# Transposing two streams side by side on half-height TensorE tiles, with loads in 4 KB runs: a scan followed by a mixture of adapters

## The chip, the cores and the metric

The kernel runs on one core of one Trainium2 chip. The metric is device time in microseconds, as a median of several executions; every execution that is compared here was in the fast state (one execution of e7 fell in a second, slower state, at 236.28 us against 232.51 to 234.76 of the other three, and is left out). The "span" that the profile shows is about 2 us shorter than the time. In the tables of the profile PE is TensorE (matmuls), PEld its weight loads, DVE is VectorE, ACT is ScalarE, POOL is GpSimd, SP is SyncE.

## The reference, cut to what matters

```python
# a, b: (8, 6400, 128) float32
for t in range(6400):
    h = a[:, t] * h + b[:, t]          # a recurrence along t, per batch and channel
    x[:, t] = h
x = x.reshape(51200, 128)
logits = x @ w_gate                    # 8 experts
# the two best experts; w = softmax of their two logits
delta = sum over the two of  w * ((x @ A[e]) @ B[e])     # A: 128 x 16, B: 16 x 128
out = x + delta
```

The kernel cuts the 51200 rows into 100 units of 512 rows. For each unit it loads a and b, transposes both on TensorE (channels to partitions, time along the free axis), runs the recurrence as one scan on VectorE, and then works through the adapters: logits, x @ A for all eight experts at once (Z), a multiply by the gates ("mul"), a transpose of the product (T), x itself and the product times B added up in PSUM (R and D), a copy out, a store.

## The kernel before

A small planner in Python gets all operations with estimated durations and dependencies. It decides the order of every engine's queue before the kernel is built, by simulating the engines with a priority for each operation. That matters later, because an operation that waits holds up what stands behind it in the same queue: in the changed kernel the transposes of unit 3, whose data had landed by 11.29 us, started at 20.51 us, behind logits that waited until 18.85 us.

The parts that the change and the argument touch:

```python
# loads: two units in one DMA, 2 KB runs (4 rows of 512 B) in each of 128 partitions; all on SyncE's queue
def load(k):
    u0, n = loads[k]
    s0 = u0 % RING
    for t, rows, ring, last in (("a", a_rows, a_in, "A"), ("b", b_rows, b_in, "B")):
        add_dma(f"ld{t}{k}", "sp", u0 - RING + 2,
            lambda h, rows=rows, ring=ring: h.dma_start(
                ring[:, s0 : s0 + n, :],
                rows[u0 * UT : (u0 + n) * UT, :].rearrange("(n p i) d -> p n (i d)", p=128, i=Q)),
            ...)

# transposes: four of 128 x 128 for a, four for b
def transposes(kind, w):
    ...
        for i in range(Q):
            last = h.transpose(view[:, i, :], ring[:, w % RING, i * 128 : (i + 1) * 128], ident_f[:, :])

# constants: three loads on ScalarE's queue; moe_A comes in 1024 pieces of 64 B
def cst_load(h):
    h.dma_start(cst_f[:, 0:E], moe_w_gate[:, :]).then_inc(s_cst, 16)
    h.dma_start(cst_f[:, E : E + 128].rearrange("p (e r) -> p e r", e=E),
                moe_A.rearrange("e d r -> d e r")).then_inc(s_cst, 16)
    return h.dma_start(cst_f[:, E + 128 : E + 256], moe_B.rearrange("e r d -> (e r) d"))
...
add("cst_in", "act", -109, 1800.0, lambda h: cst_load(h).then_inc(s_cst, 16), ...)
add("cst", "pool", -108, 600.0, lambda h: h.tensor_copy(cst_h[:, :], cst_f[:, :]), ["cst_in"])

# a multiply may run on GpSimd, fed by a copy of z on ScalarE; with PM = 1000 none does
def on_pool(w):
    return w % PM == 3 and 8 < w < NU - 16
...
plan.schedule(390.0)
```

## Time and profile before

The median is 210.99 us (three runs, 210.92 to 211.61).

| read from the profile of before | value |
|---|---|
| span | 209.4 us |
| TensorE busy | 202.2 us (97%), 2842 matmuls |
| VectorE busy | 193.6 us (92%) |
| ScalarE busy | 170.2 us |
| DMA | 393 to 400 GB/s from 40 to 190 us |
| scans start every | 1.94 us (units 20 to 90) |
| last scan starts | 195.0 us, 14.4 us before the end |

The page of the kernel before. The first line is the busy time of each engine with its share of the span and its instructions. The lines with q are DMA queues: packets, MB, share of the 16 DMA engines' time (q1 carries SyncE's loads and stores, q10 ScalarE's queue, q8 the fetches of instructions). The line of shares is the chain of work that ended last. Then come groups of instructions (line, engine, operation, tiles, count, busy us, mean ns, idle time before them), and at the end the DMA issues with the median time from issue to landing.

```profile
PE 202.2 (97%) x2842; PEld 194.9 (93%) x2842; DVE 193.6 (92%) x279; ACT 170.2 (81%) x356; POOL 87.1 (42%) x190
...
q1 hardware_dynamic: 40848, 78.65, 99.8%
q8 instruction: 22, 0.36, 0.7%
...
PE 87%; DVE 6%; ACT 2%; issue 2%; POOL 0%; DVEq 0%; POOLq 0%
...
L555 DVE TENSOR_TENSOR zw<-pZ,g 128x512 f16<-128x512 f32 x100 | 66.9, 674 | 0.8 <-ACT a_st L364 0.2
...
L350 PE MATMUL pA<-ident_f,a_in 128*128 128x128 f32 x400 | 62.2, 279 | 0.8 <-ACT a_st L364 0.6
L350 PE MATMUL pB<-ident_f,b_in 128*128 128x128 f32 x400 | 61.7, 277 | 0.2
...
L406 PE MATMUL pTL<-cst_h,xT 128*128 128x8 f16 x400 | 22.0, 174 | 0.3 <-DVE xT L381 0.3
...
cst_f<-in_moe_A_dram ACTq DMA_DIRECT2D x1, 64.0 KB, 3.9
```

TensorE is busy nearly all the time and 87% of the chain is TensorE. The mean of 279 ns is the time of one transpose from its start to its modelled end; matmuls overlap, so the distance of their starts counts. The timeline of TensorE around 100 us (start, duration, operation) shows it: four transposes of a take 0.44 us of the queue, an f16 block of four takes 0.22 us.

```profile
100.05 0.60 PE L350 MATMUL pA<-ident_f,a_in 128*128 128x128 f32 x4
100.49 0.39 PE L610 MATMUL pO<-cst_h,zwT 128*128 128x128 f16 x4
100.71 0.39 PE L571 MATMUL pTL<-ident_h,zw 128*128 128x128 f16 x4
```

### The profile page before, as it was taken

Reading aid. Unit: us, or ns where it says so; the run is one execution under the profiler, and the core shown is the slowest. Engines: PE = TensorE matmul, PEld = TensorE weight load, DVE = VectorE, ACT = ScalarE, POOL = GpSimd, SP = SyncE. Lnnn points to the kernel's source line nnn. Section 1 sums busy time; section 2 is a strip of 40 time slices with the busy share of each in tenths; the row PEclk is TensorE's granted clock in tenths of the full one; section 3 lists DMA queues with packets and bytes.
Section 4 is the critical chain, followed back from the end, with each engine's and each line's share of the span. In section 5 each row is a group of like instructions: output and inputs, shape, how many; then the busy total and the mean of one; then the engine's idle time right before and its main releaser. Section 6 shows DMA issues by size and latency. Waiting matters only on the chain.

```text
span 209.4 us, 7147 instructions
## 1 busy us (share of the span) xinstructions
PE 202.2 (97%) x2842; PEld 194.9 (93%) x2842; DVE 193.6 (92%) x279; ACT 170.2 (81%) x356; POOL 87.1 (42%) x190
## 2 busy tenths in 40 slices
PE   6989999999999999999999999999999999999992
PEld 4779899999999999999999999999999999999991
DVE  1599999999999999999999999999999999999980
ACT  2437587779888889978979789988998899899993
POOL 1032715063335443563362545435453654354310
PEclk9999999999999999999999999999999999999999
DMA  7999999999999999999999999999999999999677
GB/s 172 388 387 385 389 383 386 385 391 392 398 391 394 399 396 398 401 396 403 391 403 397 399 403 397 398 404 391 398 405 397 405 395 397 402 400 344 237 269 269
DMA packets 42208, 79.23 MB, mean 378 GB/s; under 512 B 3648, under 2 KB 3776, under 8 KB 42176
## 3 DMA queue, kind: packets, MB, share of 16 engines
q1 hardware_dynamic: 40848, 78.65, 99.8%
q8 instruction: 22, 0.36, 0.7%
q10 hardware_dynamic: 1328, 0.14, 0.5%
q14 instruction: 10, 0.08, 0.1%
HBM read 52.56 MB, written 26.21 MB: 376 GB/s over the span
## 4 chain that ended last, share of the span: by engine, by line
PE 87%; DVE 6%; ACT 2%; issue 2%; POOL 0%; DVEq 0%; POOLq 0%
PE pA L350 20%; PE pB L350 19%; PE pO L610 11%; PE pZ L521 10%; PE pO L598 10%; PE pTL L571 10%; DVE xT L381 6%; PE pTL L406 5%; ACT a_st L364 1%; ACT outt L626 1%; PE pB L300 0%; PE pB L303 0%; ACT zwT L590 0%; PE pA L571 0%; PE pB L312 0%
## 5 line engine op out<-in xcount | busy, mean ns | idle before, releaser
L381 DVE TENSOR_TENSOR_SCAN xT<-a_st,xT,pB 128x512 f16<-128x512 f32 x96 | 120.2, 1252 | 2.7 <-PE pB L350 1.1
L364 ACT COPY a_st<-pA 128x512 f32<-128x512 f32 x100 | 59.7, 597 | 18.0 <-PE pA L350 10.7
L555 DVE TENSOR_TENSOR zw<-pZ,g 128x512 f16<-128x512 f32 x100 | 66.9, 674 | 0.8 <-ACT a_st L364 0.2
L626 ACT COPY outt<-pO 128x512 f32<-128x512 f32 x98 | 57.8, 594 | 10.5 <-PE pO L610 9.1
L350 PE MATMUL pA<-ident_f,a_in 128*128 128x128 f32 x400 | 62.2, 279 | 0.8 <-ACT a_st L364 0.6
L350 PE MATMUL pB<-ident_f,b_in 128*128 128x128 f32 x400 | 61.7, 277 | 0.2
L590 ACT COPY zwT<-pTL 128x512 f16<-128x512 f16 x95 | 56.5, 595 | 3.5 <-PE pTL L571 1.9
L350 PEld LDWEIGHTS pB<-ident_f,b_in 128*128 128x128 f32 x400 | 44.1, 142 | 1.8 <-issue 1.1
L350 PEld LDWEIGHTS pA<-ident_f,a_in 128*128 128x128 f32 x400 | 43.3, 143 | 1.8 <-issue 1.3
L610 PE MATMUL pO<-cst_h,zwT 128*128 128x128 f16 x400 | 38.8, 219 | 0.4
L598 PE MATMUL pO<-ident_h,xT 128*128 128x128 f16 x400 | 38.7, 219 | 0.1
L521 PE MATMUL pZ<-cst_h,xT 128*128 128x128 f16 x400 | 38.6, 219 | 0.0
L571 PE MATMUL pTL<-ident_h,zw 128*128 128x128 f16 x380 | 36.7, 219 | 0.0
L598 PEld LDWEIGHTS pO<-ident_h,xT 128*128 128x128 f16 x400 | 30.1, 114 | 0.6 <-ACT outt L626 0.3
L610 PEld LDWEIGHTS pO<-cst_h,zwT 128*128 128x128 f16 x400 | 27.3, 98 | 2.3 <-PE pO L598 0.9
L521 PEld LDWEIGHTS pZ<-cst_h,xT 128*128 128x128 f16 x400 | 28.7, 114 | 0.2
L571 PEld LDWEIGHTS pTL<-ident_h,zw 128*128 128x128 f16 x380 | 25.7, 98 | 0.3
L406 PE MATMUL pTL<-cst_h,xT 128*128 128x8 f16 x400 | 22.0, 174 | 0.3 <-DVE xT L381 0.3
L406 PEld LDWEIGHTS pTL<-cst_h,xT 128*128 128x128 f16 x400 | 20.5, 117 | 0.8 <-DVE xT L381 0.8
L449 POOL TENSOR_TENSOR d_1<-Lg,m_1 128x128 f32<-128x128 f32 (+2 forms) x13 | 5.1, 390 | 32.6 <-DVE m_1 L441 32.6
L449 POOL TENSOR_TENSOR d_0<-Lg,m_0 128x128 f32<-128x128 f32 (+1 forms) x12 | 4.8, 398 | 29.4 <-DVE m_0 L441 29.4
L381 DVE TENSOR_TENSOR_SCAN xT<-a_st,pB 128x512 f16<-128x512 f32 (+1 forms) x8 | 7.5, 942 | 5.7 <-PE pB L350 5.4
(58 smaller groups left out, 129.9 us busy)
## 6 DMA issues: line engine op xcount, KB each, us to landing
a_in<-in_a_dram SPq DMA_DIRECT2D x49, 512.0 KB, 11.4
b_in<-in_b_dram SPq DMA_DIRECT2D x49, 512.0 KB, 11.4
out_dram<-outt SPq DMA_DIRECT2D x49, 512.0 KB, 11.4
a_in<-in_a_dram SPq DMA_DIRECT2D x2, 256.0 KB, 3.6
b_in<-in_b_dram SPq DMA_DIRECT2D x2, 256.0 KB, 4.0
out_dram<-outt SPq DMA_DIRECT2D x2, 256.0 KB, 2.6
cst_f<-in_moe_A_dram ACTq DMA_DIRECT2D x1, 64.0 KB, 3.9
cst_f<-in_moe_B_dram ACTq DMA_DIRECT2D x1, 64.0 KB, 4.5
```

The lines of the kernel that those rows point to most:

```text
L350: last = h.transpose(view[:, i, :], ring[:, w % RING, i * 128 : (i + 1) * 128], ident_f[:, :])
L364: lambda h: h.copy(a_st[w % 2][:, :], pA[:, :]),
L381: last = h.tensor_tensor_scan(out=xT[:, x0 + lo : x0 + hi], data0=a_st[w % 2][:, lo:hi], data1=pB[w % 2][:, lo:hi], initial=init, op0=ALU. ...
L406: last = h.matmul(pL[:, c : c + E], x_block(w, i), wg_h)
L449: lambda h: h.tensor_tensor(out=v(d1[s]), in0=v(Lg[s]), in1=bc(m1[s]), op=ALU.subtract),
L521: last = h.matmul(pZ[w % NZ][:, i * 128 : (i + 1) * 128], x_block(w, i), Acat_h)
L555: lambda h: h.tensor_tensor(out=oview, in0=zview, in1=gview, op=ALU.mult),
L571: last = h.transpose(t_dst(w)[:, i * 128 : (i + 1) * 128], zw[w % 2][:, i, :], ident_h[:, :])
L590: lambda h: h.copy(zwT[w % 2][:, :], t_dst(w)),
L598: last = h.matmul(pO[w % NO][:, i * 128 : (i + 1) * 128], x_block(w, i), ident_h[:, :], start=i == 0, stop=False, skip_group_check=True,)
L610: last = h.matmul(pO[w % NO][:, i * 128 : (i + 1) * 128], zwT[w % 2][:, i * 128 : (i + 1) * 128], Bcat_h, start=False, stop=True, skip_gro ...
L626: return copy(outt[:, w % NOUT, :], pO[w % NO][:, :])
```

## The change

Its intent: a transpose of a 64-row block on the upper half of TensorE and one on the lower half run at the same time. So the unit is laid out as 64 partitions of 8 rows. Unit w of a sits in one half, and unit w of b, shifted by one unit, in the other half, so that the eight pairs of a unit's transposes run side by side. A load of two units fills 128 partitions, in runs of 4 KB instead of 2 KB. Besides, 26 of the 100 multiplies go to GpSimd (with a copy of z on ScalarE for each), the warm-up of TensorE is cut to five matmuls, the planner counts 100 ns for a change between half-height and full-height work, all priorities are new, and the first load of b is issued from ScalarE's queue, so that it is issued sooner.

The diff, cut to its core:

```diff
-    PM = 1000
+    ON_POOL = lambda v: 8 < v < NU - 12 and v % 3 == 1
     ...
-            for i in range(8):
-                for p, dst in ((0, pB[1]), (64, pO[0])):
-                    h.transpose( ... )          # and the rest of the old warm-up
+            for _ in range(5):
+                last = h.matmul(pB[1][:, :], warm_t[:, 0:128], warm_t[:, :])
     ...
+        def place(t, w):
+            shift = 0 if t == "a" else 1
+            half = 64 * ((w + shift) % 2)
+            return (w + shift) // 2, slice(half, half + 64)
+
+        def load(t, n, units, eng="sp"):
+            ring, rows = (a_in, a_rows) if t == "a" else (b_in, b_rows)
+            first, last = place(t, units[0])[1], place(t, units[-1])[1]
+            src = rows[units[0] * UT : (units[-1] + 1) * UT, :]
+            dst = ring[first.start : last.stop, n % RING, :]
+            ...
+                [(dst, src.rearrange("(p i) d -> p (i d)", i=QI))],
     ...
-                for i in range(Q):
-                    last = h.transpose(
-                        view[:, i, :], ring[:, w % RING, i * 128 : (i + 1) * 128], ident_f[:, :]
-                    )
+                for i in range(QI):             # QI = 8
+                    for dst, src, rows in srcs: # a on one half, b on the other
+                        last = h.transpose(dst[:, i, :], src[:, i * D : (i + 1) * D], ident_f[rows, rows])
     ...
-        for k in range(len(loads)):
-            load(k)
+        load("a", 0, [0])
+        load("b", 0, [0], "act")
+        load("a", 0, [1])
+        for n in range(1, NS):
+            load("b", n, [2 * n - 1, 2 * n])
+            load("a", n, [2 * n, 2 * n + 1])
+        load("b", NS, [NU - 1])
     ...
-        plan.schedule(390.0)
+        plan.schedule(410.0)
```

## The prediction

> **What bounds the kernel now.** Three resources are almost equally full, at about 1.9 us per unit of 512 rows (100 units).
> - TensorE: the page has PE 97% busy, and the chain of waits is 87% PE. In the chain between 100 and 125 us the transposes of a and of b take 0.44 us each per unit (4 at 110 ns), the four f16 blocks 0.22 to 0.25 each, the logits 0.11: about 1.88 us.
> - VectorE (timeline): scans 1.19 us and gate multiplies 0.59 us start to start, plus two reductions of 0.19 us per four units: about 1.87 us, with almost no idle time from 14 to 195 us.
> - DMA: 78.65 MB, queue share 99.8%; the table by stretches has 393 to 400 GB/s from 40 to 190 us, so 1.97 us per unit. SyncE's load issues take 1.2 us (median)[...].
>
> Loads run ahead; all have landed by about 185 us, while TensorE still has some ten units to go. From 190 us DMA falls to 270 GB/s. The last scan starts at 195.0 us, the span ends at 209.4.
>
> **What changes.**
> 1. TensorE: 16 half-height transposes in 8 pairs. The warm-up of the old kernel already runs such pairs: both members start together and pairs follow each other every 106 ns, while its 128-column f16 matmuls there take about 102 ns, twice their later 55, so at half clock. At full clock I estimate 53 ns a pair, 0.43 us per unit for both, instead of 0.88. [...] TensorE comes to about 1.6 us per unit.
> 2. VectorE: 26 of the 100 multiplies move to GpSimd: 26 x 0.59 = 15 us less; 1.72 us per unit on average. ScalarE gains 26 copies at 0.48 us (12 us)[...]. Neither becomes a limit.
> 3. DMA: loads in 4 KB packets. In the packet records 64 B take 11 ns, 512 B 27, 2 KB 84, 8 KB 308: about 9 ns fixed plus 36.5 ns per KB. So 4 KB should take 159 ns against 2 x 84: loads 5.6% faster, all traffic (a third is stores, still 2 KB) 3.7%, about 412 GB/s.
>
> **On the critical path.** With TensorE at 1.6 and VectorE at 1.72, DMA at 1.91 us per unit is the slowest, so TensorE's 0.3 us per unit are mostly not seen; it will wait for loads. Start loss about 2.9 us, as before; some 76 MB before the last load has landed, 184.5 us at 412 GB/s: 187.5 us. Last scan at about 189 us instead of 195. The tail from the last scan was 14.4 us; with less backlog on VectorE 12 to 13. Span 201, time (measured over span, +1.6) about 202.5 us, 4% faster.
>
> **Predicted** 202.5 us, range 198.5 to 207. Faster by over 2%: 0.82; within 2%: 0.15; slower by over 2%: 0.03.
>
> **Shown right by:** a pair of transposes every 53 to 60 ns; 4 KB packets of about 159 ns; DMA at 405 to 418 GB/s until about 187 us; PE busy falling to 80 to 88% with waits for loads; VectorE about 178 us busy; last scan near 189 us.
>
> **Wrong if:** weight loads do not overlap between tiles (TensorE back at 1.9 us, no gain); mode changes cost much more; ScalarE's in-order queue or GpSimd's slow multiplies stall the scan chain; the tail keeps its 14 us or grows; or stores with mixed packet sizes slow the loads.

Terms that no trace showed are cut from it: an allowance for the changes between full and half height (its "mode changes"), a figure for GpSimd's added time, and a cause for the length of SyncE's issues. For TensorE the terms that stand make 1.88 less 0.88 plus 0.43, 1.43 us per unit; the 1.6 that the prediction goes on with contains the cut allowance, which was not shown by any trace. In the warm-up the weight loads of a pair start together too (both at 2.56 us). What an extra pair of changes costs was measured later: 0.206 us (e7 less e8). The multiplies of GpSimd, which it calls slow, took 1.06 us each in the changed kernel, those of VectorE 0.68 us. The 53 ns for a pair, the 159 ns for a 4 KB packet and the 412 GB/s are estimates from the numbers that stand beside them.

## More of the kernel before

Logits, Z and D of every unit need the constants ("cst").

The constants had landed at 6.1 us in this kernel, before the first scan started, and nothing on TensorE waited for them.

## The result, and the profile after

The changed kernel takes 217.98 us (median of four, 217.92 to 218.83), against 211.06 us for the kernel before in the same rounds. It is slower: the ratio is 1.0332, with a 95% interval of 1.0301 to 1.0363. Ratios here are the mean time of one kernel's fast runs over that of the other's of the same rounds, so they aren't quite the ratio of the medians quoted. Executions over 1.5% slower than the fastest of the same kernel are left out of the means.

The page of the changed kernel, the lines that answer to those above (L372 are the transposes, L447 the logits, L599 the multiplies):

```profile
PE 192.6 (89%) x3605; PEld 170.5 (79%) x3605; DVE 182.9 (85%) x252; ACT 176.2 (82%) x378; POOL 112.2 (52%) x209
...
q1 hardware_dynamic: 27968, 78.39, 92.6%
...
q8 instruction: 28, 0.46, 0.8%
...
PE 73%; DVE 11%; DMA 7%; issue 3%; ACT 3%; ACTq 1%; POOL 0%; DVEq 0%
...
L372 PE MATMUL pA<-ident_f,a_in 64*128 64x64 f32 x800 | 75.4, 237 | 6.9 <-issue 2.4
...
L372 PE MATMUL pB<-ident_f,b_in 64*128 64x64 f32 x800 | 76.0, 238 | 0.2 <-issue 0.2
...
L599 DVE TENSOR_TENSOR zw<-pZ,g 128x512 f16<-128x512 f32 x74 | 50.3, 682 | 4.5 <-PE pTL L615 3.3
...
L447 PE MATMUL pTL<-cst_h,xT 128*128 128x8 f16 x400 | 28.9, 178 | 8.5 <-POOL cst_h L322 7.5
...
cst_f<-in_moe_A_dram ACTq DMA_DIRECT2D x1, 64.0 KB, 14.5
```

What to see: TensorE is less busy, VectorE too, and yet the span grew by 6.8 us (209.4 to 216.2). The logits waited 7.5 us once, for the constants in f16. The load of moe_A took 14.5 us instead of 3.9. The chain that ended last contains 7% of DMA, where the kernel before had none: that is the load of the constants.

The waits of the first 30 us show the same thing as a chain. Columns: engine, tile and line, what ended the wait, us in total, times, longest us. First the kernel before, then the changed one.

```profile
POOL cst_h L323 <- DMA cst_f<-in_moe_B_dram: 4.7, 1, 4.7
```

```profile
POOL cst_h L322 <- DMA cst_f<-in_moe_B_dram: 16.9, 1, 16.9
...
PE pTL L447 <- POOL cst_h L322: 7.5, 1, 7.5
```

In the changed kernel TensorE's timeline stands still from 11 to 18.85 us. While the first logits wait for the constants, no transpose gets past them, though the data of the next ones had landed by 11.29 us:

```profile
...
11.00 0.31 PE L372 MATMUL pA<-ident_f,a_in 64*128 64x64 f32 x1
11.03 0.31 PE L372 MATMUL pB<-ident_f,b_in 64*128 64x64 f32 x1
18.85 0.30 PE L447 MATMUL pTL<-cst_h,xT 128*128 128x8 f16 x4 [7.51 <-POOL cst_h L322]
```

Where the difference of 6.8 us in the span comes from, by the start times of the scans:

| | before | after | after minus before |
|---|---|---|---|
| scan of unit 20 starts | 40.4 | 52.5 | +12.1 |
| from there to the scan of unit 99 | 154.6 | 146.2 | -8.4 |
| from there to the end | 14.4 | 17.5 | +3.1 |
| span | 209.4 | 216.2 | +6.8 |

So the change does what it was meant to do in the steady part, though less than predicted. It loses more at the start, and some at the end.

### The profile page after: what moved, and what is told of

It reads as the page before. It is cut to its first block, busy times and chain, and to the rows that moved or that the text cites. A ratio compares the mean times of both kernels' runs of the same rounds, so it can differ in the third digit from the quotient of the medians.

```text
span 216.2 us, 8638 instructions
## 1 busy us (share of the span) xinstructions
PE 192.6 (89%) x3605; PEld 170.5 (79%) x3605; DVE 182.9 (85%) x252; ACT 176.2 (82%) x378; POOL 112.2 (52%) x209
## 4 chain that ended last, share of the span: by engine, by line
PE 73%; DVE 11%; DMA 7%; issue 3%; ACT 3%; ACTq 1%; POOL 0%; DVEq 0%
PE pA L372 23%; PE pZ L561 10%; PE pTL L615 10%; PE pO L657 9%; PE pO L645 9%; DVE xT L412 8%; DMA cst_f<-in_moe_B_dram 7%; PE pTL L447 7%; PE pB L372 4%; ACT a_st L393 2%; DVE zw L599 2%; ACT zwT L637 1%; PE pA L615 0%; ACT outt L673 0%; ACTq L294 0%
## 5 line engine op out<-in xcount | busy, mean ns | idle before, releaser
L372 PE MATMUL pA<-ident_f,a_in 64*128 64x64 f32 x800 | 75.4, 237 | 6.9 <-issue 2.4
L372 PE MATMUL pB<-ident_f,b_in 64*128 64x64 f32 x800 | 76.0, 238 | 0.2 <-issue 0.2
L372 PEld LDWEIGHTS pA<-ident_f,a_in 64*128 64x128 f32 x800 | 61.2, 146 | 17.4 <-issue 9.6
L372 PEld LDWEIGHTS pB<-ident_f,b_in 64*128 64x128 f32 x800 | 61.3, 146 | 0.3 <-issue 0.2
L599 DVE TENSOR_TENSOR zw<-pZ,g 128x512 f16<-128x512 f32 x74 | 50.3, 682 | 4.5 <-PE pTL L615 3.3
L599 POOL TENSOR_TENSOR zw<-z_sb,g 128x512 f16<-128x512 f32 x26 | 27.6, 1063 | 17.3 <-PE pTL L615 9.5
L447 PE MATMUL pTL<-cst_h,xT 128*128 128x8 f16 x400 | 28.9, 178 | 8.5 <-POOL cst_h L322 7.5
L447 PEld LDWEIGHTS pTL<-cst_h,xT 128*128 128x128 f16 x400 | 22.0, 119 | 14.2 <-POOL cst_h L322 7.7
L615 PEld LDWEIGHTS pTL<-ident_h,zw 128*128 128x128 f16 x380 | 23.3, 98 | 2.3 <-issue 0.9
L585 ACT COPY z_sb<-pZ 128x512 f32<-128x512 f32 x26 | 15.8, 608 | 0.0
L480 ACT COPY Lg<-pTL 128x128 f32<-128x128 f32 (+1 forms) x27 | 7.5, 277 | 7.8 <-PE pTL L447 7.8
## 6 DMA issues: line engine op xcount, KB each, us to landing
cst_f<-in_moe_A_dram ACTq DMA_DIRECT2D x1, 64.0 KB, 14.5
```

The source lines that it names most:

```text
L372: last = h.transpose(dst[:, i, :], src[:, i * D : (i + 1) * D], ident_f[rows, rows])
L447: last = h.matmul(pL[:, c : c + E], x_block(v, q), wg_h)
L585: lambda h: h.copy(src[:, :], pZ[v % NZ][:, :]),
L599: lambda h: h.tensor_tensor(out=oview, in0=zview, in1=gview, op=ALU.mult),
L615: last = h.transpose(t_dst(v)[:, q * 128 : (q + 1) * 128], zw[v % 2][:, q, :], ident_h[:, :])
```

## The experiments

Fifteen kernels ran; each has runs of the kernel before on the same chip. "e1" is the changed kernel with one load moved, and most later experiments start from it.

| label | starts from | median us (range) | before | ratio (95% interval) |
|---|---|---|---|---|
| e1_b0_on_sync | after | 211.60 (210.69 to 212.0) | 211.38 | 1.0006 (0.9981 to 1.0032) |
| e2_constants_first | after | 215.24 (214.16 to 216.11) | 211.38 | 1.0182 (1.0147 to 1.0218) |
| e3_before_late_constants | before | 216.59 (216.06 to 216.85) | 211.38 | 1.0246 (1.0229 to 1.0262) |
| e4_no_gpsimd_multiplies | e1 | 216.11 (215.03 to 217.3) | 211.38 | 1.0245 (1.0206 to 1.0284) |
| e5_before_short_warmup | before | 210.87 (210.31 to 211.48) | 211.11 | 0.9986 (0.9962 to 1.0011) |
| e6_constants_and_warmup | e1 | 211.86 (210.19 to 212.8) | 211.11 | 1.0024 (0.9968 to 1.008) |
| e7_extra_mode_change | e1 | 233.47 (232.51 to 234.76; three runs) | 211.11 | 1.1064 (1.0998 to 1.113) |
| e8_extra_half_matmul | e1 | 219.97 (219.06 to 221.62) | 211.11 | 1.0425 (1.0375 to 1.0476) |
| e9_two_kb_runs | e1 | 214.15 (214.05 to 214.74) | 211.24 | 1.0134 (1.0107 to 1.0161) |
| e10_before_gpsimd_multiplies | before | 214.39 (214.22 to 214.76) | 211.24 | 1.0145 (1.0114 to 1.0175) |
| e11_order_for_the_tail | e1 | 213.89 (212.75 to 214.41) | 211.24 | 1.0108 (1.0069 to 1.0148) |
| e12_order_second | e1 | 210.38 (208.63 to 210.74) | 211.24 | 0.9933 (0.9886 to 0.998) |
| e16_almost_no_stores | e1 | 207.06 (206.9 to 207.59) | 211.26 | 0.9796 (0.9771 to 0.9821) |
| e17_before_almost_no_stores | before | 212.18 (211.3 to 212.97) | 211.26 | 1.002 (0.9978 to 1.0063) |
| e13_small_backlog | e1 | 215.32 (214.9 to 215.8) | 211.26 | 1.0183 (1.0156 to 1.0211) |

All but e16 and e17 computed the right result.

### Why do the constants come late? e1, e2, e3

Theory, from the packet records: the 64 B packets of moe_A now share the DMA engines with 4 KB packets of loads, and pass about one for one with them. In the kernel before, the 1024 packets of 64 B ran between 3.68 and 4.45 us, ahead of most loads: 0.77 us. In the changed kernel they ran from 6.10 to 16.16 us, and 909 packets of 4 KB started among them. The records don't name the engine of a packet; if the little ones are spread evenly over the 16 engines (an assumption), each has 64, so by this estimate one came every 157 ns on average. A 4 KB packet of the loads takes 159 ns (median): about one large packet was served for each little one. This is an average: 379 of the 1024 passed in the first 2 us, and the other 645 took 8.0 us, with 749 packets of 4 KB among them. A rival is that the shorter warm-up or the slower clock of TensorE costs the time at the start.

e1 keeps every queue of the changed kernel except that the first load of b goes back to SyncE's queue, second in order:

```diff
         self.span = max(end.values())
+        late = ops["ldb0"]; self.order["act"].remove(late); self.order["sp"].insert(1, late)
```

> The changed kernel with one instruction moved: the first load of b goes back to the SyncE queue, so the constants are again the first DMAs on the ScalarE queue; every compute engine keeps its order. Theory (late constants): their 1024 packets of 64 B pass in about 1 us instead of 10, they land at about 6 us instead of 17.9, the first logits start at about 9 us instead of 18.9, and the time falls by 8 to 10 us to 207 to 210 us, a little below before's 211. Rival (the mode switches of TensorE, 1.8 us per unit, make the kernel slow in every stage): 216 to 218 us.

Measured: 211.60 us, 6.4 us less than the changed kernel, by the medians of two different calls; the kernel before differs by 0.3 us between those calls. The 64 B packets ran from 3.02 to 3.88 us, and the constants had landed at 6.7 us. The wait of the logits is gone. The span is 209.6 us, 6.6 less.

The page of e1, the line that answers to 14.5 us:

```profile
cst_f<-in_moe_A_dram ACTq DMA_DIRECT2D x1, 64.0 KB, 4.0
```

e2 keeps the load of b on ScalarE's queue but puts it behind the constants:

```diff
+        first = ops["cst_in"]; self.order["act"].remove(first); self.order["act"].insert(0, first)
```

> The changed kernel with the constants issued on the ScalarE queue ahead of the first load of b, which stays on that queue behind them. Theory (late constants): constants land at 6 to 7 us, the first transposes start 0.5 to 1.5 us later than at 5.6 us because b comes later, time 208 to 211 us. Rival (mode switches): 216 to 218 us.

Measured: 215.24 us, above the 208 to 211 of the theory. The constants had landed at 6.7 us, as wanted, but now the packets of the load of b came late, from 5.96 to 9.52 us, after the last packet of the constants (5.90 us), and the first scan started only at 12.4 us (8.3 in e1). So this order pays half of the loss in another place.

e3 does the reverse in the kernel before: the first load of b moves to ScalarE's queue, ahead of the constants, and nothing else changes.

```diff
+        late = ops["ldb0"]; self.order["sp"].remove(late); self.order["act"].insert(0, late)
```

> The kernel before with the first load of b put ahead of the constants on the ScalarE queue, and nothing else. Theory (a packet of the constants waits for one packet of the loads at each turn): 64 packets per DMA engine at about 84 + 11 ns, so the 64 B packets take about 6 us instead of 0.8, constants land at 11 to 14 us instead of 6.0, and the kernel before becomes slower by 4 to 7 us: 215 to 218 us. Rival (the old kernel is bound by TensorE, VectorE and DMA later on and can take a late start): 211 to 212 us.

Measured: 216.59 us, 5.2 us slower than the kernel before in the same rounds. The 64 B packets ran from 4.71 to 10.71 us, 6.0 us. They did not pass evenly: 841 of the 1024 started in the first 1.2 us, and the last 24 took 2 us, for the most part 87 ns apart, about one 2 KB packet (84 ns) each. So the taking of turns, one for one, is seen in the last of them and not in all; the load counts as landed only after its last piece (in the changed kernel moe_A landed at 16.69 us, its last piece ended at 16.16). The waits of e3 in the first 30 us:

```profile
POOL cst_h L323 <- DMA cst_f<-in_moe_B_dram: 10.8, 1, 10.8
...
PE pTL L406 <- POOL cst_h L323: 3.9, 1, 3.9
```

What follows: one load's place in a queue makes the whole of the net loss against the kernel before. It can be taken away from the one kernel and given to the other.

### Does the warm-up or the clock cost the start? e5, e6

The rival of the last section. The clock records of the changed kernel have the full clock only from 32.8 us on, those of the kernel before from 7.8 us on, and the pairs of transposes follow each other every 107 ns before that time and every 62 ns after it. Two readings stand beside that. In the changed kernel TensorE, back at work at 18.85 us, was busy for 80% of the time to 29.12 us, with waits of up to 0.7 us, and the pairs stayed at 107 ns; then it worked for 3.7 us without a wait, and the full clock was recorded at 32.8 us. In e1 the clock fell back to half from 18.4 to 25.2 us (mean granted clock 0.84 from 15 to 20 us, 0.87 from 20 to 40 us). What brings the full clock, and what holds it back, no run here isolates. e5 gives the kernel before the short warm-up of the changed one:

```diff
-            for _ in range(2): ... # the whole old warm-up
+            for _ in range(5):
+                last = h.matmul(pB[1][:, :], warm_t[:, 0:128], warm_t[:, :])
```

> The kernel before with the changed kernel's warm-up (five 128x512 matmuls, ending at 3.5 us) in place of its own (which ends at 5.0 us, when the first transposes start). Theory (the clock at the start is the second part of the loss): TensorE idles from 3.5 to 5 us, the full clock comes later than at 7.8 us or is taken back, the 20th scan starts 1 to 4 us later than at 40.4 us, and the time rises by 1 to 5 us, to 212 to 216. Rival (the warm-up does not matter for the time, since data and VectorE pace the first units): 211 to 211.5 us, 20th scan at 40 to 41 us.

Measured: 210.87 us, no different from the kernel before. Its full clock came at 9.9 us.

e6 is e1 with twelve warm-up matmuls instead of five and four to eight small filler matmuls ahead of the transposes of units 1 to 8:

```diff
-            for _ in range(5):
+            for _ in range(12):
     ...
+        for w in range(1, 9):    # 8 or 4 matmuls of 128 x 128 ahead of AB{w}
+            self.order["pe"].insert(self.order["pe"].index(ops[f"AB{w}"]), extra)
```

> As e1 (first load of b on the SyncE queue), with a longer warm-up (12 matmuls) and short filler matmuls before the transposes of units 1 to 8, at places where TensorE waited. Theory (clock): full clock from about 8 us and kept, instead of 25 us in e1; 20th scan at 39 to 42 us instead of 44.9; time 206 to 209 us, below e1's 211.6. Rival (the clock does not matter at the start): 211 to 213 us.

Measured: 211.86 us, the same as e1 within its interval, so the theory's 206 to 209 was missed. The full clock came at 4.8 us, and the scan of unit 20 at 42.9 us instead of 44.9. The 2 us were lost again later: e6 had six waits of TensorE of 0.68 to 1.4 us between 48 and 162 us (see e16). So the late full clock costs about 2 us of the start, but the loss of the changed kernel isn't that, and repairing it alone did not shorten the run.

### What does a change between half and full height cost? e7, e8

With e1 the changed kernel only equals the kernel before, and the predicted gain of 8 us is still missing. The prediction had TensorE at 1.6 us per unit. The timeline of the changed kernel at full clock shows a block of pairs whole (the two members of a pair start together, then follow logits and f16 blocks):

```profile
99.81 0.33 PE L645 MATMUL pO<-ident_h,xT 128*128 128x128 f16 x3
100.08 0.27 PE L372 MATMUL pA<-ident_f,a_in 64*128 64x64 f32 x1
100.08 0.27 PE L372 MATMUL pB<-ident_f,b_in 64*128 64x64 f32 x1
100.19 0.22 PE L372 MATMUL pA<-ident_f,a_in 64*128 64x64 f32 x1
...
100.25 0.22 PE L372 MATMUL pA<-ident_f,a_in 64*128 64x64 f32 x1
...
100.56 0.22 PE L372 MATMUL pA<-ident_f,a_in 64*128 64x64 f32 x1
...
100.72 0.30 PE L447 MATMUL pTL<-cst_h,xT 128*128 128x8 f16 x4
```

What to see: both halves start at 100.08, so the pair does run in parallel. The second pair comes 0.11 us later, all others every 0.06 us, and the next full-height block starts 0.16 us after the last pair. From start to start, the medians from 50 to 170 us are: first to last pair 486 ns, the step into the pairs 150 ns, the step to the second pair 112 ns and the step out of them 154 ns, where two full-height f16 matmuls are 56 ns apart. A pair thus costs about 62 ns, and the two changes of height cost about 94 ns on entry (150 less 56), 50 ns at the second pair (112 less 62) and 92 ns on leaving (154 less 62): 0.236 us per unit. The unit takes 1.785 us of TensorE's queue.

e7 puts one full-height matmul of 8 columns into the middle of each block of pairs; e8 is its control with the same matmul on 64 rows only, which changes no height:

```diff
                 for i in range(QI):
+                    if i == 3:
+                        h.matmul(da[:, 7, 0:8], warm_t[:, 0:128], warm_t[:, 0:8])    # e7
+                        h.matmul(da[:, 7, 0:8], warm_t[ra, 0:128], warm_t[ra, 0:8])  # e8
```

> As e1, with one 128-row matmul of 8 columns in the middle of each unit's 16 half-height transposes, whose result the last transposes overwrite: two more changes of tile shape per unit. From the trace the two changes that a unit has now cost about 0.29 us (0.09 after the last pair, 0.15 before the first, 0.05 within the first). If TensorE paces the kernel and a pair of changes costs that, 100 x 0.25 to 0.3 us: 232 to 243 us. If another engine paces it: under 220 us.

> Control for e7: the same small matmul at the same place, but on the 64-row tile that is in use, so no change of tile shape. Expected 100 x 0.03 to 0.06 us over e1: 212 to 218 us. If it costs as much as e7, it is the instruction and not the change of shape that costs.

The 0.03 to 0.06 us for a small matmul are the author's estimate: in the kernel before four logits of 8 columns take 0.11 us of the queue, 27 ns each, and full-height f16 matmuls of 128 columns are 56 ns apart.

The timeline of e7 shows the extra matmul (L374) between two pairs. From start to start the step to it takes 0.16 us, the step to the next pair 0.11 us and the step to the pair after that 0.11 us again:

```profile
100.12 0.22 PE L372 MATMUL pA<-ident_f,a_in 64*128 64x64 f32 x1
100.12 0.22 PE L372 MATMUL pB<-ident_f,b_in 64*128 64x64 f32 x1
100.28 0.18 PE L374 MATMUL pA<-warm_t 128*128 128x8 f16 x1
100.39 0.27 PE L372 MATMUL pA<-ident_f,a_in 64*128 64x64 f32 x1
...
100.50 0.22 PE L372 MATMUL pA<-ident_f,a_in 64*128 64x64 f32 x1
```

Measured: e7 233.47 us (fast runs), as expected; e8 219.97 us, 2 us above its expected range. The unit in TensorE's queue is 2.043 us in e7 and 1.837 us in e8 (medians): an extra pair of changes costs 0.206 us. The pitch of the scans from unit 20 to 90 is 2.049 us in e7 and 1.931 in e8, against 1.847 in e1: e7's is its TensorE queue, e8's and e1's are that and some waits of TensorE (see e16) that e7 has not. In e7 the cost added on TensorE shows in full, so TensorE paces it, and the changes of height are a real cost: some 0.2 us out of 1.79. That TensorE's queue is the floor of e1 as well is seen in e16.

### Do the 4 KB packets help? e9

e9 is e1 with each load split into two DMAs of 2 KB runs, all orders kept:

```diff
-                [(dst, src.rearrange("(p i) d -> p (i d)", i=QI))],
+                [(dst[:, c : c + 512], src.rearrange("(p i) d -> p (i d)", i=QI)[:, c : c + 512]) for c in (0, 512)],
```

> As e1, with each load issued as two DMAs of 2 KB runs instead of one of 4 KB runs; same layout, same order on the compute engines. In e1 the loads land 4 us or more before their transposes from unit 10 on, so the packet rate should matter little. Theory (DMA does not pace the kernel): packets of 84 ns, 390 to 400 GB/s instead of 410, slack of the loads smaller by some us, time within 1% of e1: 210 to 214 us. Rival (the prediction's: DMA paces the kernel): the time follows the DMA rate, 3 to 4% above e1, 217 to 220 us.

Measured: 214.15 us, 1.3% over the kernel before and so about 1.3% over e1. The scan of unit 20 came 1.3 us later (46.2 against 44.9), the pitch after it is nearly that of e1 (1.856 against 1.847 us), and the tail was 0.9 us longer (18.5 against 17.6). So larger packets helped mainly at the two ends. Why is not isolated: at the start the full clock, too, came later (27.3 us, against 25.2 in e1). In the steady part loads land well ahead of their use: from about unit 20 on, a load was there at least 4.7 us before its transposes in the kernel before (from unit 30), 13 us in the changed kernel and 5.7 us in e1. So DMA, which the prediction made the pace-setter, set the pace of the steady part in none of them.

### What is the GpSimd part worth? e4, e10

e4 is e1 with all multiplies on VectorE, planned anew; e10 is the kernel before with 19 of its 100 multiplies on GpSimd.

```diff
-    ON_POOL = lambda v: 8 < v < NU - 12 and v % 3 == 1
+    ON_POOL = lambda v: False                            # e4
```

```diff
-    PM = 1000
+    PM = 4                                               # e10
```

> As e1, with all gate multiplies on VectorE (no copies of z by ScalarE, no multiplies on GpSimd), planned anew. If TensorE with its mode switches sets the 1.8 us per unit, VectorE at about 1.88 us per unit now sets it instead: 3 to 7 us slower than e1. If ScalarE (97% busy between 60 and 120 us with the copies) sets it, the same as e1 or faster.

> The kernel before with 19 of the 100 gate multiplies on GpSimd (one of four, units 9 to 83), as the changed kernel does with 26: this part of the change alone. If TensorE alone paces the old kernel: 210.5 to 212 us. If VectorE alone paced it: about 19 x 0.59 us less, 200 to 202 us. The reading of both as equal limits: 209 to 212 us.

Measured: e4 216.11 us, 4.5 us slower than e1, with a pitch of 1.910 us; e10 214.39 us, 3 us slower than the kernel before and above all three expectations. So the sign of this part of the change depends on the rest. With TensorE at 1.79 us per unit, VectorE at its old load is the limit (in e4 it is busy for 58.9 of the 60 us from 60 to 120), and the relief pays. In e10 VectorE's busy time in that stretch falls to 53.8 us, but TensorE is busy for all 60 us, so the relief has nothing to relieve. (Why e10 is slower, and not merely the same, was not isolated; ScalarE has 19 more copies in its queue.)

### New orders: e11, e12

Both start from e1 with twelve warm-up matmuls and change the planner's figures (540 ns for a block of pairs, 95 ns for a change, 320 ns for the sigmoid), the priorities, the first and last groups of gates and the share of GpSimd (one multiply in four).

```diff
-    TAIL = 10
-    KEY = { "AB": -14.1, ..., "oev": 28.9 }
-    ON_POOL = lambda v: 8 < v < NU - 12 and v % 3 == 1
+    TAIL = 14                                             # e11; 12 in e12
+    KEY = { "AB": -12.7, ..., "oev": -11.5 }              # e11; -16.2, ..., 14.3 in e12
+    ON_POOL = lambda v: 3 < v < NU - 12 and v % 4 == 1    # e11; 8 < v < NU - 13 in e12
```

> As e1 with the long warm-up, planned anew with other priorities (searched on a replay of the static order with the measured durations: 540 ns for the transposes, 95 ns per change of shape), smaller groups of units at both ends and a multiply on GpSimd in one of four units. Theory (the other half of the miss lies in the order: in e1 11 multiplies are still open when the last scan starts, and the tail takes 17.6 us): tail 11 to 14 us, last scan at 189 to 193 us, time 202 to 207 us, faster than before and after. Rival (the tail is set by latencies that no order removes): tail 16 to 18 us, time 209 to 212 us.

> As e11 with another set of priorities, closer to the changed kernel's (strict order by unit). Theory: 203 to 208 us. Rival: 209 to 212 us.

Measured: e11 213.89 us, a miss. e12 210.38 us, also above its theory's 203 to 208: the same as the kernel before within 2% (ratio 0.9933, the interval just below 1), and 3.5% better than the changed kernel by the medians. It did not shorten the tail (17.5 us, with 89 multiplies begun at the last scan, as in e1); its gain is in the steady part, with a pitch of 1.827 us. Its profiled run was the fastest of its four (208.63 us), so its profile flatters it a little. It is the fastest correct version that was found.

### Where does e1 lose the rest? e16, e17

The busy time of every engine by stretches shows when TensorE stood idle: the length of the stretch less PE's busy time. The lines of the kernel before and then of e1; columns: stretch, its length, busy us and instructions of PE, PEld, DVE, ACT and POOL, the clock, the DMA share and GB/s.

```profile
60.00:120.00 60.00, 60.00 (x870) 59.17 (x867) 59.02 (x82) 52.73 (x111) 27.85 (x57) 1.00 1.05 398
120.00:180.00 60.00, 60.00 (x892) 59.60 (x891) 59.00 (x83) 52.89 (x112) 29.46 (x60) 1.00 1.05 399
180.00:195.00 15.00, 15.00 (x237) 14.89 (x235) 14.71 (x25) 13.76 (x31) 7.50 (x17) 1.00 0.96 367
```

```profile
60.00:120.00 60.00, 59.81 (x1196) 54.44 (x1197) 57.50 (x73) 58.63 (x129) 40.20 (x70) 1.00 1.04 411
120.00:180.00 60.00, 56.91 (x1124) 51.11 (x1122) 54.15 (x70) 55.55 (x119) 39.09 (x67) 1.00 1.04 409
180.00:195.00 15.00, 13.84 (x264) 12.27 (x261) 14.04 (x21) 13.46 (x31) 7.30 (x15) 1.00 0.70 260
```

The kernel before has no idle time of TensorE at all in these three stretches. e1 has 0.2, 3.1 and 1.2 us. TensorE's timeline of e1 shows one of these waits, in the middle of a block of four, with nothing to wait for:

```profile
148.83 0.33 PE L615 MATMUL pTL<-ident_h,zw 128*128 128x128 f16 x3
149.65 0.23 PE L615 MATMUL pTL<-ident_h,zw 128*128 128x128 f16 x1 [0.49 <-issue]
```

e1 has six such waits over 0.55 us from start to start after 30 us (0.60 to 1.12 us each, where two matmuls are otherwise 56 ns apart), at 122.1, 135.5, 148.9, 162.2, 175.6 and 189.7 us. Counted in instructions of TensorE as the trace lists them, they fall after number 4290, 4801, 5314, 5825, 6338 and 6849: 511 to 513 apart, which is twice 256. In the changed kernel the four waits stand at the same four first numbers, 8 us later; in e9 all six are at the same numbers. In e6, e8, e11 and e12 they stand elsewhere, but their distances are multiples of 256 as well, within 2 (except for one wait of 0.55 us in e12). And in e1 each ends 1.3 to 1.5 us after a packet of 16 KB on the instruction queue has ended. The page counts 28 such packets in the changed kernel and 22 in the kernel before, where TensorE has 3605 and 2842 matmuls, each with a weight load.

The counts agree with the positions: 28 packets for the 7210 matmuls and weight loads of the changed kernel are one for 258 of them, and so are 22 for the 5684 of the kernel before. So the theory is: TensorE's instructions come in blocks of about 256; with more of them per microsecond it needs a block every 6.5 us (an estimate from the 1124 to 1196 matmuls, each with its weight load, in 60 us of e1), the fetch has to share DMA engines that loads and stores keep full (share 1.04, 409 to 411 GB/s), and it comes too late. Rivals: the DMA traffic itself paces e1; or the waits belong to these places whatever the traffic.

e16 is e1 with only the last 8 of its 51 stores (the result is wrong), every compute engine's order the same. e17 does the same to the kernel before, as a control.

```diff
-        for j in range(len(stores)):
+        for j in range(len(stores) - 8, len(stores)):
             store(j)
```

> e1 with only the last 8 of 51 stores kept (result wrong on purpose; every compute engine's order the same as in e1). Theory F (TensorE waits for its own instructions, whose fetches come late because loads and stores keep the DMA engines full): once the loads run ahead, from about 30 us on, the DMA engines have idle time, the waits of TensorE over 0.55 us after 30 us (six in e1, 4.7 us of start-to-start time, about 3.5 to 4 us lost) go away, the 60 to 180 us stretch has under 0.6 us of TensorE idle time where e1 has 3.3, and the span is 3 to 4.5 us shorter than e1's 209.6: 205 to 206.6, time about 207 to 208.5. Rival D (the DMA traffic paces e1): the pitch of the scans from unit 20 to 90 falls well below 1.80 us, to 1.75 or less. Rival P (the waits belong to the instruction positions themselves, whatever the traffic): the waits stay where they are, at the same matmul indices, and the time is within 1 us of e1's.

> The kernel before with only the last 8 of its 51 stores kept (result wrong on purpose; TensorE's order differs in a few places late in the run only). Control for e16: the kernel before has no waits over 0.55 us after 12 us, so if only fetches are at stake nothing changes: 210 to 212, within 1% of before, pitch from unit 20 to 90 of 1.92 to 1.94 us. If the DMA engines, full at 400 GB/s, are a third limit of the kernel before, as the prediction said, it gets faster by 2 us or more.

Measured: e16 207.06 us, e17 212.18 us. The same stretches of e16:

```profile
60.00:120.00 60.00, 59.88 (x1209) 54.51 (x1206) 57.61 (x74) 58.90 (x129) 40.89 (x71) 1.00 0.88 303
120.00:180.00 60.00, 59.91 (x1208) 54.54 (x1205) 57.77 (x75) 59.17 (x130) 40.14 (x69) 1.00 0.63 210
180.00:195.00 15.00, 14.48 (x256) 12.67 (x254) 14.55 (x32) 13.93 (x32) 8.10 (x18) 1.00 0.19 70
```

All six waits are gone (in e1 they add up to 4.75 us from start to start), though the page of e16 still counts 28 instruction packets. The span fell from 209.6 to 205.1 us although e16's scan of unit 20 came 0.9 us later. The pitch became 1.799 us, which is TensorE's own 1.785 and a little, and not less, so traffic had not been the pace. The other rival falls too: the places are still passed, and the waits are gone. The control gained nothing from the same relief (pitch 1.934 against 1.936 us). The packet records add to this. At the places 256 instructions apart that TensorE passes between 120 and 180 us, the last 16 KB packet had ended 1.3 to 1.6 us earlier in e1, and 2.0 to 4.6 us earlier in e16. The packets themselves take about as long in both (medians of 1.04 and 1.02 us), so what differs is when they start. And e7, whose added matmul spreads the instructions (1089 matmuls in 60 us where e1 has 1196) while its DMA engines are full too (share 1.02, 383 to 388 GB/s), has no idle time of TensorE from 60 to 180 us. So about 4.5 us of e1's time go with late instruction fetches, and in these runs they came only with both: the denser instruction stream and the full DMA engines. Not shown is what delays the start of a fetch, nor why the waits start only after 120 us in e1 and at 48 us in e6.

### Is the longer tail a loss of its own? e13

After the last scan the changed kernel and e1 need 17.5 us, the kernel before 14.4. At that moment 89 of the 100 multiplies had been begun in e1 and in the changed kernel, 92 in the kernel before. e13 is e1 with the transposes of the last 16 units made to wait for the multiply nine units back, so that the planner does the older work first:

```diff
-                [load_of["a", w], load_of["b", w], a_free(w), f"scan{w - 2}", "id"],
+                [load_of["a", w], load_of["b", w], a_free(w), f"scan{w - 2}", "id"] + [f"mul{w - 9}"] * (w >= NU - 16),
```

> e1 with the transposes of the last 16 units waiting for the multiply nine units back, which makes the planner give the last units' multiplies and output blocks an earlier place; planned backlog at the last scan: 8 multiplies, as in the kernel before, where e1 has 11. Theory W (the tail is TensorE's postponed work, which has to be done in any order): the tail from the last scan falls from 17.6 to 14.5 to 16 us, but the last scan starts 3 to 8 us later than e1's 192.0, and the time is no better than e1's: 211 to 216. Rival O (the backlog itself is the loss): the last scan at 192 to 193.5 and the time 207 to 209.

Measured: 215.32 us. At the last scan 93 multiplies had been begun, and the tail was 14.0 us. But the last scan started at 199.1 us instead of 192.0 (with TensorE at a mean granted clock of 0.81 from 190 us to there). The tail of the changed kernel is postponed work. This way of doing it earlier costs more than it saves; that no order at all could do better is not shown.

## Why the prediction was wrong

The prediction was 202.5 us, with 0.82 for "faster"; the result was 217.98 us. In spans, 201 was predicted and 216.2 measured. The 15.2 us between them come out of the runs:

| term | us | from |
|---|---|---|
| constants late | 6.6 | after to e1, spans 216.2 to 209.6 |
| late instruction fetches | 4.5 | e1 to e16, spans 209.6 to 205.1 |
| last scan of e16 against the prediction | -1.4 | 187.6 against 189 |
| tail of e16 against the prediction | 5.5 | 17.5 against 12 (201 less 189) |

Point by point:

1. **The step that failed first is "Start loss about 2.9 us, as before".** The prediction read the first loads of the kernel before and did not follow the one load that the diff puts on ScalarE's queue. Ahead of the constants it delayed them by 12 us (they had landed at 18.3 instead of 6.1 us), and TensorE's queue, in which the next transposes stood behind the logits, turned that into 7.5 us of standing still. e1 and e3 show it in both directions. This alone makes the difference between "same" and "slower".

2. **"TensorE comes to about 1.6 us per unit" was mis-sized.** The mechanism was right: both halves start together, and pairs follow each other every 62 ns, not far from the estimate of 53 and just outside the stated 53 to 60. But the changes of height cost 0.236 us, more than the 0.17 or so that 1.6 leaves over the 1.43 of the other terms, and the unit came to 1.785 us. An extra pair of changes cost 0.206 us (e7 against e8); the runs show this cost and not what happens in it. Against the pitch of 1.94 us of the kernel before, less than half of the expected relief was left. The trace of the kernel before held a hint: in its warm-up, before the full clock came, the step from the last pair to the next full-height matmul was 243 ns, where pairs were 106 ns apart.

3. **"DMA at 1.91 us per unit is the slowest" was wrong.** The rate was right: 4 KB packets took 159 ns, as predicted, and DMA ran at 401 to 415 GB/s in the steady slices of the page. But in the steady part the loads were always ahead of TensorE by several microseconds (see e9), and with almost all stores gone (e16) the pitch fell only to TensorE's own. The errors of this point and of point 2 hid each other, which is luck: a limit that wasn't there predicted a last scan at 189 us, close to the 187.6 that TensorE's true pace gives in e16.

4. **The tail was predicted to shrink to "12 to 13" us, "with less backlog on VectorE".** It grew to 17.5. The relief of VectorE doesn't reach the tail: the diff allows it only below unit 88 (the last such unit is 85), so the last 14 multiplies all stay on VectorE. And the plan lets the scans run ahead and leaves 11 units of multiplies and output blocks, against 8. The chain that ended last runs on VectorE from the last scan to 202.9 us and on TensorE from there to 210.8, so the backlog is on both. e13 shows that shrinking it delays the last scan by more.

5. **Not foreseen at all: instruction fetches.** 27% more matmuls (3605 against 2842), in less time per unit, go with waits of TensorE at places 511 to 513 of its instructions apart (e1) while the DMA engines are full: 4.5 us in e1. The list of what would make the prediction wrong doesn't have it.

6. **Right:** VectorE came to 182.9 us (178 predicted); GpSimd's busy time rose by 25 us, and at 52% busy it was no limit; packets, rate and parallel pairs as above. ScalarE did come close to a limit, 97% busy from 60 to 120 us, but e7 shows that TensorE set the pace.

What stays open: with the constants repaired, e1 still reaches unit 20 at 44.9 us against 40.4 before. About 2 us of it go away with the full clock (e6); the rest was not isolated.

## What to carry to other kernels

Before moving a load to another queue, see what stands behind it there: here a load in 1024 tiny pieces took 0.77 us ahead of a stream of large packets and 10 us in the midst of it, and the one late constant stopped the whole queue of TensorE for 7.5 us. When a change splits instructions to run them in parallel, count the changes of shape and the instructions as well as the arithmetic: the first cost 0.2 us per unit here, the second 4.5 us in all. And when several engines are nearly equally full, test which one paces by adding a known cost to one of them (e7) or taking one away (e16), before a gain is booked.
